# Earlier decay loads and scans, smaller constants, shared masks and a new order in a state-space layer with a GELU MLP

## The chip, the cores and the metric

The kernel runs on one core of a Trainium2 chip. The metric is the device time of one execution in microseconds (us); less is better. The profile is one execution taken by the hardware profiler. Engines are TensorE (PE; its weight loads PEld), VectorE (DVE), ScalarE (ACT), GpSimd (POOL) and SyncE (SP), the last of which only issues transfers here.

## The reference, cut to what matters

Four sequences of 768 steps, 8 heads, head size 32, state size 16. Each head runs a state-space recurrence with a decay `a` per step; its output, regrouped to 3072 tokens of 256 numbers, goes through an MLP with GELU (256 to 2048 to 256). Per chunk of steps:

```python
log_a = np.log(np.clip(a, 1e-06, 1.0))
cum = np.cumsum(la, axis=-1)
L = np.exp(cum[:, :, :, None] - cum[:, :, None, :]) * causal
M = np.einsum('bhin,bhjn->bhij', Cc, Bc) * L
y = M @ xc + (Cc @ state) * exp(cum)
state = exp(sum(la)) * state + sum_j B_j x_j * exp(cum[-1] - cum_j)
...
h = x @ w_in
g = 0.5 * h * (1.0 + np.tanh(c * (h + 0.044715 * h * h * h)))
out = g @ w_out
```

Inputs and output are float32; inside, matmul operands are bf16.

## The kernel before, in words

A chunk is 128 steps, so there are 24 chunks (`gc` or `c`), six to a sequence, handled as 12 pairs (`u`). There are no loops that set the order: every piece of work is a named `Step`, and the string `ORDERED` at the top lists all steps in the order in which they are issued. `name:A`, `:D`, `:P`, `:S` choose ScalarE, VectorE, GpSimd or SP for a step that allows it, and `~n` puts in fill matmuls of `n` x 128 zero columns that only keep TensorE busy. Each engine runs its own steps in that order and waits where it needs another's result. SP holds nearly all loads and stores, in list order too. Buffers are few: two PSUM banks `hp` (first-layer results, also used for state products), one `o_ps`, one `yb`, and two pairs `ga`, `gb` for the score matrices.

**Decays.** Rather than logarithms the kernel scans products. For batch 0's first four chunks `aq_t` holds 128 decays per row; `f_clipq` clips them, `f_Rq` (L331) scans from the end of the chunk, `f_tpq` (L342) turns the result, `f_recip0` (L348) inverts it. `f_mulb` (L416) and `f_mulc` (L409, two halves by parity of the head) multiply B and C by these, TensorE transposes them (`f_tw`), `f_ew` copies them to SBUF. All other chunks use `a_t` (rows of 384 decays): `f_clip`, `f_R`, `f_tp2`, `f_tp6`, `f_recip`. `f_peq`/`f_ppq`/`f_pendq` and `f_pe`/`f_pp`/`f_pend` make the whole-chunk decays through a small matmul with the selector `selp`.

**Per pair.** `G.u` makes the scores C B of both chunks into `ga` and `gb` (L595). `M.u.0` and `M.u.1` (L605, VectorE) multiply them by the triangular mask `tri`. In pair 0 the second half goes another way: `GE.g` (L610, ScalarE) copies one bank `gb` to SBUF, `ME.g` (L616, GpSimd) cuts it with an affine select. `D.u` (or `XD.u`, L573, in pairs 0 and 1) makes the state update, `S.u.k` (L674, L676) adds it to the decayed state, `SP.c` (L683) spreads the state over a block mask as the operand of the next chunk. `Y.u` (L650 and L659) sums both parts into `yb`, and `yev.u` copies it to `xm`. In pairs 0 and 1 x comes as `x4_t` with four steps to a row; `XX.u` (L563) spreads it with the constant `unp`.

**MLP.** `s1.u.i` (L709) makes 256 of 2048 hidden units for the pair's 256 tokens, with two weight halves; `gelu.u.i` (L713, ScalarE) applies GELU; `s2.c.q` (L727) adds a quarter of the second layer for a chunk; `oev.c` copies and `store.c` stores the result. The weights arrive as float32 in four quarters each (`load_wi.q`, `load_wo.q`, 512 KB each) and are cast in halves by `wi.q.k` and `wo.q.k` on any of three engines (the copies of L314, L316, L318). A group `s1.u.i` needs quarter `i // 2` of w_in, `s2.c.q` needs quarter `q` of w_out.

The constants `ident`, `tri`, `m8`, `bmask` and `cz` (zeros that `f_mulc` fills by halves) come from GpSimd, `wz`, `ends`, `unp`, `selp`, `m4` and `par` from VectorE.

Of the kernel before, what the change touches and what calls it, by code (L numbers as in the profile page):

```python
# [8 lines left out]
FP32 = mybir.dt.float32  # L9
BF16 = mybir.dt.bfloat16  # L10
# [77 lines left out]
def kernel(  # L88
# [53 lines left out]
    def a_rows(t, n):  # L142
        return bass.AP(tensor=a.tensor, offset=a.offset + t, ap=[[S, batch * H], [1, n]])
# [14 lines left out]
    def load_aq(i, eng):  # L158
        (nc.scalar if eng == "ACT" else nc.sync).dma_start(out=aq_t[32 * i:32 * i + 32], in_=a_rows(i * Q, Q))  # L159
# [93 lines left out]
    def c_cz():  # L253
        nc.gpsimd.memset(cz, 0.0)
# [708 lines left out]
```

## Time and profile before

| | |
|---|---|
| times of the runs shown | 116.7, 116.92, 117.4 us; median 116.92 |
| span of the profiled execution, first to last instruction | 115.1 us |
| instructions in it | 3372 |
| bytes read and written | 11.04 MB, 3.93 MB |
| VectorE busy | 68.7 us in 135 instructions |
| ScalarE busy | 75.1 us in 149 |
| GpSimd busy | 15.1 us in 32 |

The profiled execution is known by its span. The times of the runs include what lies before the first and behind the last instruction as well: 1.8 us for the median. A row of a timeline has start, duration, engine, line, operation, output and inputs, number of instructions, and in brackets how long the engine had been idle before it and who ended that. A row of a stretch has for each engine busy time and number of instructions, then the granted TensorE clock, the share of the 16 DMA engines and GB/s. Lines are those of the kernel before.

### The profile page before, as it was taken

To read this page: it belongs to the slowest core of one execution; us is meant where nothing else is said; L and a number is where in the kernel's file an instruction comes from. 1 tells how busy PE (TensorE), PEld (TensorE's weight loads), DVE (VectorE), ACT (ScalarE), POOL (GpSimd) and SP (SyncE) were. 2 spreads that over 40 slices of the span, in tenths; PEclk is the share of its full clock that TensorE was granted. 3 is DMA by queue.
4 is the path that set the end of the run, shared out by engine and by line. 5 is a ranking of instruction groups with operands and counts; after the bars stand their busy time and mean duration, and the time that the engine had idled before them with its cause. 6 is when DMAs were issued, how large, how long until landed. Compare 5 with 4: busy or idle time off the path is not lost.

```text
span 115.1 us, 3372 instructions
## 1 busy us (share of the span) xinstructions
PE 109.4 (95%) x1425; PEld 92.2 (80%) x1425; DVE 68.7 (60%) x135; ACT 75.1 (65%) x149; POOL 15.1 (13%) x32
## 2 busy tenths in 40 slices
PE   6999799999999999999999999999999999999990
PEld 2354578978877979799898998998989989999970
DVE  6688799998799989196966281546827421000100
ACT  3119889978657767657576486377766765685710
POOL 6564274122220000020002000000000000000000
PEclk9999999999999999999999999999999999999999
DMA  2999999949969828959478760000014014001132
GB/s 65 236 280 286 397 293 311 278 84 218 225 109 226 214 64 203 192 147 265 102 158 184 174 178 0 6 0 0 0 50 138 0 49 139 0 0 51 46 103 79
DMA packets 43006, 15.97 MB, mean 139 GB/s; under 512 B 36656, under 2 KB 41456, under 8 KB 42992
## 3 DMA queue, kind: packets, MB, share of 16 engines
q1 hardware_dynamic: 42848, 15.68, 53.9%
q8 instruction: 11, 0.18, 0.6%
q10 hardware_dynamic: 144, 0.08, 0.4%
q14 instruction: 3, 0.02, 0.1%
HBM read 11.04 MB, written 3.93 MB: 130 GB/s over the span
## 4 chain that ended last, share of the span: by engine, by line
PE 82%; DMA 8%; SPq 4%; POOL 1%; issue 1%; ACT 0%
PE hp L709 36%; PE o_ps L727 33%; DMA wf<-in_moe_w_out_dram 8%; PE yb L727 3%; PE ga L595 3%; PE yb L650 2%; PE yb L659 2%; SPq L190 1%; PE hp L628 1%; SPq L162 1%; SPq L159 1%; SPq L150 1%; POOL w_out_sb L316 1%; POOL w_in_sb L316 1%; SPq L183 1%
## 5 line engine op out<-in xcount | busy, mean ns | idle before, releaser
L713 ACT ACTIVATE gT<-hp 128x512 bf16<-128x512 f32 x96 | 53.3, 595 | 24.5 <-PE hp L709 24.0
L709 PE MATMUL hp<-xm,w_in_sb 128*128 128x256 bf16 x384 | 51.9, 273 | 0.5 <-ACT pend L314 0.3
L727 PE MATMUL o_ps<-w_out_sb,gT 128*128 128x256 bf16 x352 | 46.4, 273 | 0.0
L709 PEld LDWEIGHTS <-w_in_sb 128*128 128x128 bf16 x384 | 41.2, 114 | 3.2 <-issue 1.7
L727 PEld LDWEIGHTS <-gT 128*128 128x128 bf16 x384 | 37.0, 98 | 4.7 <-issue 0.8
L318 DVE COPY o_sb<-o_ps 128x256 f32<-128x256 f32 x7 | 3.0, 424 | 22.4 <-PE o_ps L727 18.4
L605 DVE TENSOR_TENSOR m<-ga,tri 128x1024 bf16<-128x1024 f32 x12 | 14.6, 1216 | 0.0
L605 DVE TENSOR_TENSOR m<-gb,tri 128x1024 bf16<-128x1024 f32 x11 | 13.4, 1219 | 0.5 <-PE gb L595 0.5
L697 PE MATMUL yb<-wz 128*128 128x512 bf16 (+2 forms) x24 | 8.2, 491 | 1.1 <-DVE warm L222 1.1
L314 ACT ACTIVATE o_sb<-o_ps 128x256 f32<-128x256 f32 x15 | 5.6, 382 | 4.1 <-PE o_ps L727 3.0
L683 DVE SCALAR_TENSOR_TENSOR sp_new<-s_new,pend,bmask 128x256 bf16<-128x256 f32 x17 | 8.0, 479 | 0.1
L316 POOL CAST x<-x_t 128x512 bf16<-128x512 f32 x5 | 3.2, 648 | 34.9 <-DMA x_t<-in_x_dram 22.9
L676 DVE SCALAR_TENSOR_TENSOR s_new<-s_new,pend,hp 128x64 f32<-128x64 f32 x13 | 3.6, 279 | 5.7 <-PE hp L628 5.5
L697 PEld LDWEIGHTS <-wz 128*128 128x128 bf16 x25 | 2.9, 126 | 5.0 <-issue 3.6
L659 PE MATMUL yb<-m,x 128*32 128x128 bf16 x192 | 6.1, 219 | 0.0
L650 PE MATMUL yb<-ce,sp_new 128*32 128x128 bf16 x160 | 5.3, 220 | 0.0
L595 PE MATMUL ga<-ce,bh 32*128 32x256 bf16 x48 | 4.7, 272 | 0.1
L314 ACT ACTIVATE xm<-yb 128x512 bf16<-128x512 f32 x8 | 4.8, 597 | 0.0
L595 PE MATMUL gb<-ce,bh 32*128 32x256 bf16 x48 | 4.7, 273 | 0.0
L727 PE MATMUL yb<-w_out_sb,gT 128*128 128x256 bf16 x32 | 4.1, 273 | 0.0
L659 PEld LDWEIGHTS <-x 128*32 128x32 bf16 x192 | 3.8, 97 | 0.4 <-issue 0.2
L650 PEld LDWEIGHTS <-sp_new 128*32 128x32 bf16 x160 | 3.0, 96 | 1.0 <-issue 1.0
(108 smaller groups left out, 78.4 us busy)
## 6 DMA issues: line engine op xcount, KB each, us to landing
out_dram<-o_sb SPq DMA_DIRECT2D x24, 128.0 KB, 2.0
x_t<-in_x_dram SPq DMA_DIRECT2D x20, 128.0 KB, 3.8
wf<-in_moe_w_in_dram SPq DMA_DIRECT2D x4, 512.0 KB, 8.3
wf<-in_moe_w_out_dram SPq DMA_DIRECT2D x4, 512.0 KB, 8.9
bc_t<-in_B_dram SPq DMA_DIRECT2D x3, 384.0 KB, 4.8
bc_t<-in_C_dram SPq DMA_DIRECT2D x3, 384.0 KB, 4.3
scr<-bc SPq DMA_DIRECT2D x4, 192.0 KB, 3.1
x_t<-in_x_dram SPq DMA_DIRECT2D x1, 512.0 KB, 4.8
```

Of the source, the lines that this page charges most:

```text
L314: nc.scalar.activation(o, i, AF.Copy)
L316: nc.gpsimd.tensor_copy(out=o, in_=i)
L595: nc.tensor.matmul(out=gbank(g)[:, 256 * k:256 * k + 256], lhsT=bh_of(2 * u + k)[gs], rhs=ce_of(2 * u + k)[gs], start=True, stop=True, til ...
L605: nc.vector.tensor_tensor(out=m_of(u)[:, 2 * i:2 * i + 2].rearrange("p g k e t -> p (g k e) t"), in0=gx[i].rearrange("p g (k t) -> p (g k) ...
L650: nc.tensor.matmul(out=y4[32 * j:32 * j + 32, k, w], lhsT=sp[:, 32 * h:32 * h + 32], rhs=ce_of(gc)[:, h % 2], start=first(j), stop=False, ...
L659: nc.tensor.matmul(out=y4[32 * j:32 * j + 32, k, w], lhsT=X16[u][:, k, 32 * h:32 * h + 32], rhs=m[:, h // 2, h % 2, :], start=first(j), st ...
L676: nc.vector.scalar_tensor_tensor(out=s_new, in0=state[("s", gc - 1)], scalar=pend_of(gc), in1=d, op0=ALU.mult, op1=ALU.add)
L683: nc.vector.scalar_tensor_tensor(out=sp_new.rearrange("p (g d) -> p g d", g=4), in0=(XN[0][:, H * D:H * D + 64] if gc == 0 else state[("s" ...
L697: nc.tensor.matmul(out=t[:, 0:m * 128], lhsT=wz, rhs=w3.to_broadcast([128, m, 128]), start=True, stop=True, skip_group_check=True)
L709: nc.tensor.matmul(out=hp[:, j * T:(j + 1) * T], lhsT=w_in_k[:, w, q, k], rhs=xm[:, w, u * T:(u + 1) * T], start=(w == 0), stop=(w == 1))
L713: nc.scalar.activation(gts[u][:, 2 * i:2 * i + 2], hps.pop((u, i)).rearrange("p (j t) -> p j t", j=2), AF.Gelu_apprx_tanh)
L727: nc.tensor.matmul(out=ops[gc], lhsT=gts[u][:, fi, k * Q:(k + 1) * Q], rhs=w_out_sb[:, fi, :], start=(fi == 0 and (u > 0 or k == 0)), stop ...
```

## The change

The new list orders nearly every step anew. Beside the order it does this:

- `aq_t` is loaded by two transfers of 64 rows, both on ScalarE's queue, in place of four of 32 rows (two on ScalarE's queue, two on SP's). Rows that nobody reads now hold other decays. `load_a.0` and `load_a.1` are SP's first two transfers, ahead of C, B and x; `load_a.0` was on ScalarE's queue.
- SP's order of the weights was wi0 wi1 wi2 wo0 wi3 B1 wo1 C1 wo2 wo3 (B1, C1: batch 0's last two chunks); it becomes wi0 wi1 wi2 wo0 C1 B1 wo1 wi3 wo2 wo3.
- The clip of `a_t` stands ahead of `recip0`, and its scan `R`, with `pe` and `tp2`, stands ahead of pair 0's masks. The first half of C's products goes to GpSimd.
- `unp` is cleared by a step of its own and filled by one strided copy in place of four.
- Pair 1 gets the same treatment as pair 0: `GE.1.2`, `GE.1.3` on ScalarE, `ME.1.3` on GpSimd, `ME.1.2` on VectorE.
- `SP.3`, `SP.6`, `SP.7`, `SP.8`, `SP.10` are made by GpSimd in two instructions.
- `s1.1.0` no longer depends on `s1.0.7`, and pair 1's groups are interleaved with pair 0's.
- The fill matmuls are `~39 ~5 ~5 ~5 ~3`; they were `~53 ~9 ~8 ~2 ~13` and a `+4` ahead of `s1.0.2`.
- Both casts of w_in's first quarter are on GpSimd (they were on ScalarE), and both of w_out's third quarter (they were on ScalarE and GpSimd).

```diff
+GEU = (0, 1)
 ORDERED = """
+c_wz load_aq.0:A load_a.0:S load_aq.1:A c_ident c_unp0:D c_zero c_warm c_unp c_sel c_m4 clipq
+load_a.1:S Rq tpq clip load_bc0.1 recip0 peq ~39 ppq pendq:A c_bmask c_tri c_cz:P c_m8 mulc.0:P ~5
+tw.1 ew.1.1:A ew.0.1:A R mulc.1:D ~5 tw.2 pe tp2 load_bc0.0 mulb:P tw.0 ew.0.2:A ew.0.0:A load_x4
+x4.1:P pp G.0 x4.0:D ew.1.2:A ew.1.0:A load_wi.0 load_wi.1 ~5 XX.0 XD.0 recip1 M.0.0 xn.0:D SP.0
+S.0.0 GE.0.2 ME.0.2:P GE.0.3 G.1 xn.1:A GE.1.3 pend:A GE.1.2 ME.0.3:P ~3 Y.0 yev.0.0.2:A load_wi.2
+load_wo.0 load_bc1.1 load_bc1.0 load_wo.1 load_wi.3 load_wo.2 load_wo.3 load_bc.1.1 load_bc.1.0
+load_x.2 load_x.3 wi.0.1:P wi.0.0:P ME.1.3:P wi.1.0:P wi.2.1:P wi.2.0:P wo.0.0:P wo.0.1:P wi.1.1:A
+S.0.1 M.1.0 XX.1 XD.1 S.1.0 ME.1.2:D S.1.1 SP.1:D SP.2:D c_par tp6.2 mul1.1 mul1.0 SP.3:P tp6.1
+wo.1.1:P xn.2:A s1.0.0 gelu.0.0 xn.3:A s1.0.1 gelu.0.1 s1.0.2 gelu.0.2 Y.1 s1.0.3 yev.1.0.2:A
+gelu.0.3 s1.0.4 gelu.0.4 s2.0.0.0.o s1.1.0 gelu.1.0 s2.0.1.0.o T1.1 T1.0 s1.0.5 s1.1.1 wi.3.1:P
+ce1.0:A tp6.3 wo.1.0:D ce1.1:D wi.3.0:D gelu.0.5 bh1:A s2.0.0.1.o s1.1.2 G.2 gelu.1.1 wo.2.0:P
+wo.2.1:P gelu.1.2 s1.0.6 wo.3.0:P wo.3.1:P gelu.0.6 s1.0.7 s2.0.1.1.o gelu.0.7 s1.1.3 gelu.1.3
+s2.0.0.2.o tp6.0 M.2.0 s1.1.4 s1.1.5 N1 s2.0.1.2.o gelu.1.4 bn1:A s1.1.6 s2.0.0.3.o gelu.1.5
...
     def load_aq(i, eng):
-        (nc.scalar if eng == "ACT" else nc.sync).dma_start(out=aq_t[32 * i:32 * i + 32], in_=a_rows(i * Q, Q))
+        (nc.scalar if eng == "ACT" else nc.sync).dma_start(
+            out=aq_t[64 * i:64 * i + 64],
+            in_=bass.AP(tensor=a.tensor, offset=a.offset + 8 * P4 * i, ap=[[P4, 8], [S, H], [1, Q]]))
...
-        for r in range(R4):
-            nc.vector.tensor_copy(out=unp[:, r, :, r], in_=sub)
+        d = unp[:, 0, :, 0]
+        diag = bass.AP(tensor=d.tensor, offset=d.offset, ap=[list(d.ap[0]), [Q + 1, R4], [R4, P4]])
+        nc.vector.tensor_copy(out=diag, in_=sub.rearrange("p (o q) -> p o q", o=1).to_broadcast([128, R4, P4]))
...
-    def f_SP(gc):
+    def f_SP(gc, eng):
         sp_new = st.tile([128, 256], BF16, name="sp_new")
+        if eng == "POOL":
+            sc = spf[gc % 2]
+            nc.gpsimd.tensor_scalar(out=sc, in0=state[("s", gc)], scalar1=pend_of(gc + 1), scalar2=None, op0=ALU.mult)
+            nc.gpsimd.tensor_tensor(out=sp_new.rearrange("p (g d) -> p g d", g=4),
+                                    in0=sc.rearrange("p (o d) -> p o d", o=1).to_broadcast([128, 4, 64]),
+                                    in1=bmask.rearrange("p (g d) -> p g d", g=4), op=ALU.mult)
+            state[("sp", gc)] = sp_new
+            return
...
-        if u:
+        if u not in GEU:
             Mn[u].append(add("D", f_M, u, 1, deps=[g, ctri]))
...
-                s.deps.append(s1.get((u - 1, NI - 1)))
+                s.deps.append(s1.get((u - 1, NI - 1)) if u > 1 else None)
```

138 lines of the change are left out of this document (67 added, 71 removed).

## The prediction

> **What bounds the kernel now.** I read the page's busy times first, then the chain of work that ended last.
>
> ```profile
> PE 109.4 (95%) x1425; PEld 92.2 (80%) x1425; DVE 68.7 (60%) x135; ACT 75.1 (65%) x149; POOL 15.1 (13%) x32
> PE 82%; DMA 8%; SPq 4%; POOL 1%; issue 1%; ACT 0%
> ```
>
> The chain is TensorE (PE) for 82% of the span; the DMA's 8% is one w_out quarter, and nothing else matters. So the question is when TensorE becomes busy for good. The stretches view, cut at the first MLP matmul and at the last hole, says it:
>
> ```profile
> core 0: us, PE busy (x) PEld busy (x) DVE busy (x) ACT busy (x) POOL busy (x), PEclk, DMA share, GB/s
> 14.18:17.51 3.33, 2.83 (x23) 2.24 (x22) 3.33 (x6) 3.03 (x7) 2.29 (x4) 1.00 1.04 286
> 17.51:112.07 94.56, 94.56 (x1243) 84.03 (x1243) 54.90 (x95) 64.58 (x125) 5.58 (x9) 1.00 0.50 118
> ```
>
> From 17.51 to 112.07 us TensorE is busy for all 94.56 us. The change alters no useful matmul, so the time can only move by what TensorE loses before that point, by a new hole behind it, or by fewer costly switches. Before it the timeline of PE has these rows:
>
> ```profile
> 9.08 0.28 PE L595 MATMUL ga<-ce,bh 32*128 32x256 bf16 x2
> 12.27 0.30 PE L659 MATMUL yb<-m,x 128*32 128x128 bf16 x8
> 14.18 1.03 PE L709 MATMUL hp<-xm,w_in_sb 128*128 128x256 bf16 x8 [0.28 <-ACT pend L314]
> 15.67 1.03 PE L709 MATMUL hp<-xm,w_in_sb 128*128 128x256 bf16 x8
> 16.54 0.60 PE L727 MATMUL o_ps<-w_out_sb,gT 128*128 128x256 bf16 x4
> 16.98 0.27 PE L709 MATMUL hp<-xm,w_in_sb 128*128 128x256 bf16 x1
> 18.39 0.29 PE L650 MATMUL yb<-ce,sp_new 128*32 128x128 bf16 x8
> ```
>
> and the chain, later, has these two pieces:
>
> ```profile
> 41.84 0.56 PE hp L709 x4
> 42.39 0.87 PE o_ps L727 x8
> ```
>
> The first useful MLP matmul (s1.0.0) starts at 14.18. Eight MLP matmuls take 0.87 us in a full stream, so one takes 0.109 us. Up to 17.51 come 8 + 8 + 4 + 1 = 21 of them, 2.3 us of work in 3.33 us: **1.0 us is lost** after the start, and all until 14.18 is start-up.
>
> **What the start consists of.** The decay chain of batch 0, from the DVE, POOL and ACT timelines:
>
> ```profile
> 2.41 0.94 POOL L254 MEMSET cz<- 128x1024 bf16 x1
> 2.41 1.25 DVE L271 TENSOR_REDUCE sel<-ident 128x8 f32<-128x128 bf16 x1
> 5.16 0.23 DVE L328 TENSOR_SCALAR acq<-aq_t 128x128 f32<-128x128 f32 x1 [0.89 <-DMA aq_t<-in_a_dram]
> 5.42 0.42 DVE L331 TENSOR_TENSOR_SCAN rq_t<-acq,ends 128x128 f32<-128x128 f32 x1
> 6.37 0.34 DVE L348 RECIPROCAL pt<-rt 128x32 f32<-128x32 f32 x1
> 6.37 1.05 POOL L416 TENSOR_TENSOR bc0s<-bcf,rt 128x512 bf16<-128x512 f32 x1 [1.74 <-DVE rt L342]
> 6.80 1.24 DVE L409 TENSOR_TENSOR cz<-bcf,pt 128x256 bf16<-128x256 f32 x2
> 9.51 1.23 DVE L605 TENSOR_TENSOR m<-ga,tri 128x1024 bf16<-128x1024 f32 x1
> 9.55 1.09 ACT L610 ACTIVATE ge<-gb 128x512 bf16<-128x512 f32 x2
> 11.60 0.94 DVE L331 TENSOR_TENSOR_SCAN r_t<-ac,ends 64x384 f32<-64x384 f32 x1
> 11.78 1.15 ACT L314 ACTIVATE w_in_sb<-wf 128x512 bf16<-128x512 f32 x2 [0.19 <-DMA wf<-in_moe_w_in_dram]
> 12.82 0.18 DVE L387 TENSOR_TENSOR pe<-pe,m 64x24 f32<-64x24 f32 x1
> 12.83 0.37 ACT L314 ACTIVATE x<-hp 128x256 bf16<-128x256 f32 x1
> 13.10 0.59 ACT L314 ACTIVATE xm<-yb 128x512 bf16<-128x512 f32 x1
> 13.16 0.61 POOL L316 CAST w_in_sb<-wf 128x512 bf16<-128x512 f32 x1 [1.72 <-DMA wf<-in_moe_w_in_dram]
> 18.14 0.99 DVE L342 STREAM_TRANSPOSE rt<-r_t 32x64 f32<-32x64 f32 x4
> ```
>
> VectorE waits 0.89 us for the fourth decay load. Its reduction of 2.41 lasts 1.25 us because the fill of cz runs on GpSimd beside it until 3.35; I read that as the two sharing a way to memory.
>
> **The change, part by part.**
>
> *Decay loads.* Two loads on ACT's queue replace two there and two on SP's; all of a goes ahead of C, B, x. The issues before:
>
> ```profile
> 0.80 0.91 ACTq L159 DMA_DIRECT2D aq_t<-in_a_dram  x2
> 1.32 1.03 SPq L159 DMA_DIRECT2D aq_t<-in_a_dram  x2
> ```
>
> SP's second aq load left at about 1.8 (two in 1.03 from 1.32) and the data were used at 5.16. The last one now leaves on ACT as that queue's second issue, at about 1.25 (two in 0.91 from 0.80), half a us sooner, with nothing large ahead of it: ready at 3.5 to 4.5. C leaves behind two a_t issues, about 1.0 us later; for that second only the small loads flow, and I estimate that C, B, x and all weights shift by 0 to 0.8 us and take 0.4.
>
> *Constants.* Three of four copies into unp go, and the clearing of unp is first. VectorE is then free at about 3.1 instead of 4.27, but GpSimd's fill of cz now stands behind ident, bmask and tri, at some 3.1 to 4.05, right where the clip would run. I take the clip at 4.05 (as early as 3.5 if the two don't clash).
>
> *Scans early.* In front of recip0 now stands the clip of the whole a (0.35 by its row, quoted below), behind it the long scan, 0.94. From the clip of 5.16 to the end of recip0 were 1.55 us; with 0.1 to 0.35 more it ends at 5.7. GpSimd then makes half of C's products (half of 1.05 for half the elements, say 0.6, to 6.35) and B's (1.05, to 7.4). VectorE scans to 6.85 and makes the other half of C's, 0.62 of the 1.24 that both took, somewhat stretched beside GpSimd: to 7.7. B's products are done at 7.4, as in the old trace at 7.42; so the transposes and G.0 win almost nothing (8.9 against 9.08). Then pe (two steps of 0.18 at most), tp2 (row 18.14) and x4.0 (0.4, a cast of 512 columns) hold M.0.0 to 9.65 against 9.51. **So the 1.1 us that the loads win are spent on the early scan.** What it buys comes later: pe, pend and the 0.94 scan no longer stand between Y.0 and s1.0.0.
>
> *Masks.* M.0.0 ends at 10.9, G.1 follows; SP.0 (0.48, a row below), behind xn.0 (0.37), ends at 11.7, so Y.0 starts at 11.75 (12.27 before). ScalarE now also makes the copies of pair 1 (2 x 0.55, as in the 9.55 row) and pend ahead of Y.0's copy: it is free at 12.6, and xm is done at 13.2 (13.69 before). For pair 1 VectorE drops a mask of 1.23 us and takes a 128x512 mask from SBUF, 0.43 (its cast of that size, below) to 0.61 (half of 1.23); GpSimd takes about 0.61, as for its casts. So Y.1 goes from 18.4 to about 15.6.
>
> *First quarter of w_in.* Its casts go from ScalarE (two in 1.15) to GpSimd, one behind the other: landing 11.8 + 0.4, then 2 x 0.61, gives 13.4. That and xm (13.2) set s1.0.0 at **13.4, 0.8 us sooner**.
>
> *Between start and saturation.* From 13.4 ScalarE has the cast of w_in's second quarter (0.6), xn.2 (0.37), gelu.0.0 (0.55) and xn.3 in a row, and s1.0.1 waits for xn.2 (0.5), s1.0.2 for a gelu (0.2), s2.0.0.0 for GpSimd's two casts of w_out's first quarter (0.35): about 1.1 us lost against 1.0: **+0.1**. Pair 1's s1 no longer waits for pair 0's last; that is what fills TensorE while weights come in.
>
> *GpSimd's SP steps.* SP.3, 6, 7, 8, 10 leave VectorE.
>
> ```profile
> L683 DVE SCALAR_TENSOR_TENSOR sp_new<-s_new,pend,bmask 128x256 bf16<-128x256 f32 x17 | 8.0, 479 | 0.1
> ```
>
> On GpSimd each is two steps; by 1.05 for 512 columns I estimate 0.7 against 0.48. Between SP.3's input and Y.2, its user, stand 28 groups of four MLP matmuls in the new order, and the others have several: cost nothing, and 0.2 to 0.5 us each if that cover were gone.
>
> *Order behind.* The new order has one block fewer in which TensorE goes to the small tiles and back (13 instead of 14 from the first s1 on). The 41.84 piece, four s1 matmuls behind such a block, took 0.56 us against 0.44 in the stream; with as much on entering: **-0.2**.
>
> *The third quarter of w_out.* This is the place where the gain can be lost.
>
> ```profile
> 0.00:19.50 19.50, 16.83 (x226) 9.82 (x227) 15.69 (x46) 12.00 (x27) 10.67 (x25) 1.00 0.90 263
> 9.23 0.35 DVE L328 TENSOR_SCALAR ac<-a_t 64x384 f32<-64x384 f32 x1
> 15.80 0.43 DVE L318 CAST w_out_sb<-wf 128x512 bf16<-128x512 f32 x1
> 22.61 0.61 POOL L316 CAST w_out_sb<-wf 128x512 bf16<-128x512 f32 x1 [3.21 <-DMA wf<-in_moe_w_out_dram]
> 23.67 1.92 PE L727 MATMUL o_ps<-w_out_sb,gT 128*128 128x256 bf16 x16
> ```
>
> It landed at 22.6, was cast by two engines and used at 23.67, with no hole. The work that stands ahead of that use is the same in the new order, less N1 (0.11). From 13.4: 12 s1 and 4 s2 groups (16 x 0.44 = 7.0), Y.1, T1, G.2 and their switches (1.3, estimated from the blocks' sizes), 1.1 lost: TensorE arrives at 22.8. The same loads stand ahead of that quarter as before, 5.14 MB with it (w_in 2.10, three quarters of w_out 1.57, x 0.52, B and C 0.79, a 0.16), and 263 GB/s had moved 5.13 MB by 19.5; so its landing is not bandwidth, and could be anything from 19.9 to 23.0 with the shift of 0.4. Both casts are now GpSimd's, 1.22 us. I take 21.8, between, so 23.0: **+0.2**.
>
> *Sum:* -0.8 + 0.1 - 0.2 + 0.2 = **-0.7 us**, 114.4 of span against 115.1. The median of the runs shown is 116.92, 1.8 above that span; I carry the difference over: **116.2 us**.
>
> **The rivals.**
>
> *The gain is used up at the start* (no change). If the fill of cz clashes longer, or C's and B's products on both engines stretch each other (one of VectorE's two took twice the other), or the weights shift by the full 0.8, s1.0.0 starts at 13.9 to 14.2 and with the block saved the time is 116.5 to 116.9; I say 116.8. For it speaks that G.0 wins nothing in my sum.
>
> *TensorE waits for w_out's third quarter* (slower). From a landing of 22.6 + 0.4 and two casts in line it starts s2.0.0.2 at 24.2 instead of 23.67, with N1 still to do: +0.65, less the 0.2 of the block: 117.4; a landing one more us late gives 118.4. It decides from a landing of about 22.5 on. For it: that quarter did land at 22.6, and small 128-byte pieces of C and B now stand ahead of w_out's second quarter. Against: three us of that landing were not bandwidth.
>
> *TensorE's clock stays low.* The fills at the start:
>
> ```profile
> 1.05 5.76 PE L697 MATMUL yb<-wz 128*128 128x512 bf16 x14 [1.05 <-DVE warm L222]
> 10.40 0.88 PE L697 MATMUL yb<-wz 128*128 128x512 bf16 x4
> ```
>
> 14 take 5.76 us, 0.41 each, and later four take 0.88, 0.22 each: half speed first, though the clock column says 1.00. The change cuts the first fill to ten, 4.2 us, with holes behind it. If speed comes only after s1 has run for some us, the 3.5 us from 13.4 on do half their work: +1.7 on the forecast, 117.9. [...]
>
> **Chances.** Forecast 0.45 (its own range 115.6 to 116.6); used up at the start 0.25; w_out 0.20; clock 0.10. About 0.5%, 0.6 us, is what a measurement of this kernel can tell from no change. The forecast's 0.45 is faster for 0.37 and same for 0.08; the first rival same for 0.19, faster and slower for 0.03 each; w_out slower for 0.18, same for 0.02; the clock slower. Faster 0.40, same 0.29, slower 0.31. Range **115.5 to 118.0**: down to s1.0.0 at 12.7 (no shift, no clash), up past the w_out case and the clock's.
>
> **What would show it.** Right: first clip at about 4.0; s1.0.0 at 13.2 to 13.6; Y.1 near 15.6; s2.0.0.2 at 22.8 to 23.2 with a hole of at most 0.3 us before it; TensorE full from there. Wrong: s1.0.0 at 13.9 or later; a hole at s2.0.0.2 released by GpSimd's cast; fills or small matmuls at half speed beyond 7 us; a hole before Y.2 or a later Y released by an SP step.

## The result and the profile after

The changed kernel took **120.21 us** (median of 4 runs, 119.36 to 120.47) beside 117.16 for the kernel before on the same chip (116.70 to 117.43): 2.7% slower, ratio 1.0271 with a 95% interval of 1.0212 to 1.0329. The forecast was 116.2 and the range ended at 118.0. The profiled execution spans 118.5 us, against 115.1. Medians here and below count every execution, and some kernels have executions over 1.5% slower than their own fastest, so the spread is given where a reading needs it.

First the stretches view of the changed kernel (columns as in the prediction: busy time of PE, PEld, DVE, ACT, POOL with instruction counts, then the granted TensorE clock, DMA share, GB/s):

```profile
4.00:6.00 2.00, 0.72 (x4) 0.16 (x2) 0.31 (x2) 0.15 (x1) 0.54 (x4) 1.00 1.13 253
6.00:8.00 2.00, 0.57 (x3) 0.55 (x4) 1.97 (x6) 0.00 (x0) 0.64 (x1) 0.83 1.04 291
8.00:10.00 2.00, 1.86 (x13) 1.01 (x11) 1.90 (x4) 0.81 (x3) 2.00 (x3) 0.50 0.99 272
...
18.00:20.00 2.00, 2.00 (x32) 1.28 (x33) 1.94 (x6) 1.73 (x4) 1.92 (x4) 0.50 0.87 225
20.00:22.00 2.00, 2.00 (x32) 1.60 (x25) 1.96 (x4) 1.42 (x4) 1.21 (x3) 0.75 0.96 368
22.00:24.00 2.00, 2.00 (x23) 1.93 (x22) 1.04 (x3) 1.70 (x4) 1.28 (x3) 1.00 1.06 358
```

From 4 to 8 us TensorE is busy for 1.29 us of 4; then the clock falls to 0.50 and stays there until it rises again between 20 and 22, though from 8 on PE reads as 93 to 100% busy. The trace's clock records give the edges: half speed from 7.33 to 20.98 us. PE's timeline has the same in durations:

```profile
1.04 3.68 PE L717 MATMUL yb<-wz 128*128 128x512 bf16 x10 [1.04 <-DVE wz L223]
7.43 0.59 PE L368 MATMUL hp<-peq,selp 128*128 128x4 f32 x2 [2.71 <-DVE peq L363]
11.20 0.39 PE L607 MATMUL ga<-ce,bh 32*128 32x256 bf16 x2
14.67 0.40 PE L671 MATMUL yb<-m,x 128*32 128x128 bf16 x8
16.74 2.79 PE L729 MATMUL hp<-xm,w_in_sb 128*128 128x256 bf16 x12
19.46 0.40 PE L662 MATMUL yb<-ce,sp_new 128*32 128x128 bf16 x8
27.05 0.60 PE L747 MATMUL o_ps<-w_out_sb,gT 128*128 128x256 bf16 x4
```

The ten fills end at 4.72, and TensorE then waits 2.71 us for VectorE's peq. G.0 comes at 11.20 (9.08 before), Y.0 at 14.67 (12.27), s1.0.0 at 16.74 (14.18), Y.1 at 19.46 (18.39). Twelve MLP matmuls take 2.79 us, 0.23 each, where a full stream needs 0.109. The last row is s2.0.0.2: it has no bracket, so it waited for nothing.

Why peq is late stands in the timelines of ACT's queue and SP's queue, of DVE and of POOL:

```profile
0.79 1.84 ACTq L161 DMA_DIRECT2D aq_t<-in_a_dram x2
```

```profile
0.79 0.86 SPq L166 DMA_DIRECT2D a_t<-in_a_dram x2
1.71 0.51 SPq L152 DMA_DIRECT2D bcf<-in_C_dram x1
```

```profile
5.65 0.23 DVE L340 TENSOR_SCALAR acq<-aq_t 128x128 f32<-128x128 f32 x1 [2.64 <-DMA aq_t<-in_a_dram]
7.29 0.94 DVE L343 TENSOR_TENSOR_SCAN r_t<-ac,ends 64x384 f32<-64x384 f32 x1
8.16 0.78 DVE L421 TENSOR_TENSOR cz<-bcf,pt 128x256 bf16<-128x256 f32 x1
8.87 1.00 DVE L397 TENSOR_TENSOR pe<-ac,r_t 64x3 f32<-64x3 f32 x1
9.97 0.47 DVE L399 TENSOR_TENSOR pe<-pe,m 64x24 f32<-64x24 f32 x1
11.99 1.16 DVE L617 TENSOR_TENSOR m<-ga,tri 128x1024 bf16<-128x1024 f32 x1
```

```profile
7.36 1.30 POOL L421 TENSOR_TENSOR cz<-bcf,pt 128x256 bf16<-128x256 f32 x1 [2.67 <-DVE pt L360]
8.62 1.23 POOL L428 TENSOR_TENSOR bc0s<-bcf,rt 128x512 bf16<-128x512 f32 x1
```

The first clip runs at 5.65, not at 4.05: the two loads took 1.84 us to issue (1.19 and 0.62 singly), so the second left at 1.98, behind C's of 1.71. And two pairs of rows overlap in a telling way. GpSimd's product starts at 7.36 inside VectorE's scan (7.29 to 8.23) and ends 0.43 us behind that scan; VectorE's pe, 64x3, starts at 8.87 inside GpSimd's product (8.62 to 9.85) and ends 0.02 behind it, 1.00 us for what took 0.15 before.

How much of the end this explains can be counted in the timelines: MLP matmuls that had started by 22, 30 and 100 us are 53, 108 and 659 of 768 before, and 24, 90 and 629 after. At 22 us 29 are missing, at 30 us 18 (the new order puts other work elsewhere), at 100 us 30: 30 x 0.109 = 3.3 us, nearly all of the difference of the spans, 3.4 us. Behind 22 us TensorE has no hole and full clock in both kernels (busy for 93.00 of 93.00 us from 22 to 115 in the changed one, for 94.56 of 94.56 from 17.51 to 112.07 before, the clock at 1.00), so **all of it is lost by 22 us.**

### The profile page after: what moved, and what is told of

Read it like the earlier page. It is cut to its first block, busy times and chain, and to the rows that moved or that the text cites. A ratio compares the mean times of both kernels' runs of the same rounds, so it can differ in the third digit from the quotient of the medians.

```text
span 118.5 us, 3369 instructions
## 1 busy us (share of the span) xinstructions
PE 111.5 (94%) x1417; PEld 93.2 (79%) x1417; DVE 67.4 (57%) x128; ACT 73.9 (62%) x145; POOL 25.7 (22%) x48
## 4 chain that ended last, share of the span: by engine, by line
PE 90%; DMA 3%; POOL 1%; DVE 1%; ACTq 1%; issue 1%; ACT 0%; DVEq 0%
PE hp L729 38%; PE o_ps L747 33%; PE ga L607 4%; DMA aq_t<-in_a_dram 3%; PE yb L747 3%; PE yb L671 3%; PE yb L662 3%; PE yb L717 1%; POOL cz L421 1%; ACTq L161 1%; PE hp L437 1%; PE hp L575 1%; PE o_ps L575 1%; PE hp L640 1%; PE hp L405 0%
## 5 line engine op out<-in xcount | busy, mean ns | idle before, releaser
L729 PE MATMUL hp<-xm,w_in_sb 128*128 128x256 bf16 x384 | 53.2, 279 | 0.0
L747 PE MATMUL o_ps<-w_out_sb,gT 128*128 128x256 bf16 x352 | 47.0, 273 | 0.0
L729 PEld LDWEIGHTS <-w_in_sb 128*128 128x128 bf16 x384 | 41.7, 115 | 3.1 <-issue 1.2
L617 DVE TENSOR_TENSOR m<-gb,tri 128x1024 bf16<-128x1024 f32 x10 | 12.1, 1212 | 0.2 <-PE gb L607 0.2
L717 PE MATMUL yb<-wz 128*128 128x512 bf16 (+2 forms) x17 | 6.3, 511 | 1.0 <-DVE wz L223 1.0
L671 PE MATMUL yb<-m,x 128*32 128x128 bf16 x192 | 6.8, 235 | 0.0
L703 DVE SCALAR_TENSOR_TENSOR sp_new<-s_new,pend,bmask 128x256 bf16<-128x256 f32 x12 | 5.7, 478 | 0.1
L717 PEld LDWEIGHTS <-wz 128*128 128x128 bf16 x17 | 2.0, 137 | 3.9 <-issue 2.7
L328 POOL CAST w_out_sb<-wf 128x512 bf16<-128x512 f32 x7 | 4.7, 696 | 0.9 <-DMA wf<-in_moe_w_out_dram 0.9
L697 POOL TENSOR_SCALAR spf<-s_new,pend 128x64 f32<-128x64 f32 x5 | 2.4, 475 | 10.9 <-DVE s_new L688 7.1
```

The source lines that it names most:

```text
L328: nc.gpsimd.tensor_copy(out=o, in_=i)
L617: nc.vector.tensor_tensor(out=m_of(u)[:, 2 * i:2 * i + 2].rearrange("p g k e t -> p (g k e) t"), in0=gx[i].rearrange("p g (k t) -> p (g k) ...
L671: nc.tensor.matmul(out=y4[32 * j:32 * j + 32, k, w], lhsT=X16[u][:, k, 32 * h:32 * h + 32], rhs=m[:, h // 2, h % 2, :], start=first(j), st ...
L703: nc.vector.scalar_tensor_tensor(out=sp_new.rearrange("p (g d) -> p g d", g=4), in0=(XN[0][:, H * D:H * D + 64] if gc == 0 else state[("s" ...
L717: nc.tensor.matmul(out=t[:, 0:m * 128], lhsT=wz, rhs=w3.to_broadcast([128, m, 128]), start=True, stop=True, skip_group_check=True)
L729: nc.tensor.matmul(out=hp[:, j * T:(j + 1) * T], lhsT=w_in_k[:, w, q, k], rhs=xm[:, w, u * T:(u + 1) * T], start=(w == 0), stop=(w == 1))
```

## The experiments

Four theories: (1) TensorE's clock, lost in the start-up's holes; (2) decays that land later, not sooner; (3) a longer start-up chain on VectorE and GpSimd; (4) the new order of weights and pieces of B and C on SP. A fifth came up on the way: (5) a later load, `bn`. Numbers behind a ratio are its 95% interval. Each set of runs stands beside its own runs of the kernel before (medians 117.06, 117.10, 117.29, 117.22 and 117.42). "Half speed" is by the clock records of the profiled execution. Diffs show the pieces of `ORDERED` that change.

**E1, a longer first fill in the changed kernel.**

```diff
-peq ~39 ppq
+peq ~75 ppq
```

> The changed kernel with one number changed: the first fill has 75 units of 128 columns in place of 39, so that TensorE has work nearly until the selector matmul at 7.4 us. Theory 1 (clock): most of the 3 us lost comes from TensorE at half clock from 7.3 to 21.0 us, entered because it had nothing to do from 4.7 to 7.4 us. Then the granted clock stays at 1.0, the first MLP matmul comes at about 15.0 us in place of 16.74, and the time is 117.3 to 118.3 us. Theory 2 (late decays) and theory 3 (products on GpSimd and the early scan are slower than forecast) leave the clock out: then the time stays within 0.5 us of 120.2.

119.89 us, 1.0229 (1.0183 to 1.0274). The first hole shrinks from 2.71 to 0.87 us, but holes of 0.61, 0.30 and 0.28 follow, and the clock falls at 10.59 instead of 7.33, until 20.83; s1.0.0 at 16.68. Covering one hole only moves the fall.

**E2, the first decays as four old loads, all on ScalarE's queue**

```diff
-            out=aq_t[64 * i:64 * i + 64],
-            in_=bass.AP(tensor=a.tensor, offset=a.offset + 8 * P4 * i, ap=[[P4, 8], [S, H], [1, Q]]))
+            out=aq_t[32 * i:32 * i + 32],
+            in_=bass.AP(tensor=a.tensor, offset=a.offset + i * Q, ap=[[S, batch * H], [1, Q]]))
...
-load_aq.1:A c_ident
+load_aq.1:A load_aq.2:A load_aq.3:A c_ident
```

> The changed kernel with aq_t loaded by four transfers of 32 rows of the old form, all four on ScalarE's queue; the rest as in the changed kernel. Theory 2 (late decays): the two transfers of 64 rows take longer to issue and to land; with the old form the first clip starts at about 4.6 us in place of 5.65, and all behind it, the first MLP matmul too, comes 0.8 to 1.1 us sooner: 119.1 to 119.4 us with the clock still low from about 7 to 20 us. If theory 1 also feeds on this (the hole on TensorE shrinks from 2.7 to 1.7 us), the clock may stay up and the time falls to 117.5 or less. If the form of the load doesn't matter, 120.2 us.

120.13 us, 1.0275 (1.0234 to 1.0316); clip at 5.97, later still. The four issues took 1.97 us. So it isn't the form of the loads; the theory as expected here fell.

**E3, both of these (first fill 65).**

> Both edits: four transfers of 32 rows on ScalarE's queue, and a first fill of 65 units. Theories 1 and 2 together: clock 1.0, first MLP matmul at about 14.0 us, time 116.3 to 117.2 us. If theory 3 (GpSimd's product at 1.30 us where 0.6 was forecast, VectorE's small step held up to 1.0 us beside it) weighs more, it stays 0.5 us or more above the kernel before, at 117.7 to 118.3 us.

119.51 us, 1.021 (1.012 to 1.0301); the profiled execution 118.64, with half speed only from 15.27 to 18.68 and s1.0.0 at 15.79, though its clip came at 6.01. Of the four executions the two with this mean clock (0.985) took 118.6 and 118.7, the others (0.957) 120.3 and 121.0: clock and time go together.

**E4, the old kernel with a short first fill.**

```diff
-peq ~53 ppq
+peq ~30 ppq
```

> The kernel before with one number changed: its first fill has 30 units in place of 53, so that TensorE has nothing to do from about 4.3 us to its selector matmul at 6.7 us. Theory 1: the clock falls or never rises in the start-up, TensorE runs at half clock until the MLP matmuls have been dense for some us, and the time is 118.5 to 120 us. Theories 2 and 3: the order and the loads are the old ones, so the time stays at 117.2 us.

118.41 us, 1.0124 (1.0067 to 1.0181): a hole of 2.04 us at 4.4, full clock only from 9.98, s1.0.0 at 14.99. **This alone, with every load and step in its old place, costs 1.35 us.**

**E5, the changed kernel with fills in every hole of the start.**

```diff
-peq ~39 ppq
+peq ~80 ppq
...
-mulc.0:P ~5 tw.1 ew.1.1:A ew.0.1:A R mulc.1:D ~5 tw.2
+mulc.0:P ~14 tw.1 ew.1.1:A ew.0.1:A R mulc.1:D ~10 tw.2
...
-x4.1:P pp G.0
+x4.1:P ~5 pp G.0
...
-load_wi.1 ~5 XX.0
+load_wi.1 ~13 XX.0
...
-GE.0.3 G.1
+GE.0.3 ~5 G.1
...
-ME.0.3:P ~3 Y.0
+ME.0.3:P ~10 Y.0
```

> The changed kernel with fill matmuls in every hole that the runs so far showed ahead of the first MLP matmul: first fill 80 instead of 39 columns of 128, and 14, 10, 5, 13, 5, 10 where it has 5, 5, none, 5, none, 3. No useful work is moved. Theory 1 (the clock falls because TensorE idles in the start-up, and the half clock from 7.3 to 21 us is most of the 3 us): TensorE stays at full clock from some 4 to 7 us on, s1.0.0 starts at 15.6 to 15.8 instead of 16.7, and the time is 117.5 to 118.3, 2 us or more below the changed kernel. Theory 3 (the start-up chain is longer by itself, and the clock only follows it): s1.0.0 still at 16.2 or later, 119.3 to 120.2. Both can hold in part: what is left above 117.1 at full clock belongs to the chain.

The profiled execution took 117.41 us at full clock from 5.07 to the end, with s1.0.0 at 14.94: the clock can be held. It is the fastest of the six, though; the others took 118.87 to 121.3, the median is 119.45, 1.0212 (1.0158 to 1.0265). Four of these others have a mean clock of 1.00 too, but that alone doesn't say that it was held (E9 reads 1.00 with half speed until 18.43). E11's profile does: 119.06 us at full clock from 4.90. So something else costs time as well; E6, E11 and E12 show a part of it.

**E6, E5 with both of C's products on VectorE and the long scan, its transposes and pend late.**

```diff
-Rq tpq clip load_bc0.1 recip0
+Rq tpq load_bc0.1 recip0
...
-mulc.0:P ~14 tw.1 ew.1.1:A ew.0.1:A R mulc.1:D ~10 tw.2 pe tp2 load_bc0.0 mulb:P tw.0 ew.0.2:A ew.0.0:A load_x4
+load_bc0.0 mulc.0:D mulc.1:D mulb:P ~10 tw.1 tw.0 ew.0.0:D ew.0.1:A tw.2 ew.0.2:A load_x4
...
-XD.0 recip1 M.0.0 xn.0:D SP.0 S.0.0 GE.0.2
+XD.0 clip M.0.0 xn.0:D SP.0 S.0.0 R pe GE.0.2
```

> As the run with fills in every hole, and beside that both of C's products are on VectorE again and the long decays' clip, scan, pe, transposes and pend stand late, as in the kernel before (clip and scan after XD.0 and S.0.0, tp2 after SP.2). Theory 3 (GpSimd's product of 1.3 us ahead of B's, and VectorE's pe held beside GpSimd, cost the start some 1.5 us): bc0s is done about 1.2 us sooner after recip0, G.0 at 9.6 to 10.0 instead of about 11, s1.0.0 at 14.4 to 14.9, and the time is 0.8 to 1.5 us below the run with fills alone. If the early scan and the split were not what is late: the same time within 0.3 us.

119.39 us, 1.0221 (1.0169 to 1.0273): no gain. This version put the small product of pe on TensorE ahead of s1.0.0, and it waited 1.35 us for VectorE there, and s1.0.0 came at 16.13; at 51 us it waits another 1.24 for a load (the row stands at E11). What the run does show is the chain ahead of that: from the clip (5.42) to G.0 (9.85) 4.43 us, against 5.25 in E5 (5.15 to 10.40). **GpSimd's product and the early scan cost G.0 0.82 us** in these two profiles.

**E7, E6 with the decays loaded as in the kernel before.**

```diff
-load_aq.0:A load_a.0:S load_aq.1:A c_ident
+load_aq.2:A load_bc0.1 load_aq.1:S load_aq.3:S load_aq.0:A c_ident
...
-clipq load_a.1:S Rq tpq load_bc0.1 recip0 peq ~80
+clipq load_bc0.0 load_x4 Rq tpq load_a.0:A load_a.1:S recip0 peq ~64
```

> As the run with fills, products on VectorE and the late scan, and beside that the decays are loaded as in the kernel before (C first on SP, four loads of 32 rows over both queues, the long decays behind the transposes); first fill 64. Theory 2 (the decays come later in the changed kernel because both of its loads wait in ScalarE's queue): first clip at 5.0 to 5.3 instead of 5.65, s1.0.0 0.4 to 0.6 us sooner than in the run without this, and the time 0.3 to 0.6 below it. If the way they are loaded is worth nothing: the same clip within 0.1 and the same time within 0.3.

119.63 us, 1.0221 (1.0178 to 1.0264). The clip came at 4.98, 0.44 sooner, and s1.0.0 0.43 sooner, as expected; the time did not follow, with half speed from 17.07 to 20.49 behind the same 1.35 us hole. At 51 us TensorE waits 0.27 us for the same load as in E6.

**E8, E5 with the old order of weights.**

```diff
-load_bc1.1 load_bc1.0 load_wo.1 load_wi.3 load_wo.2
+load_wi.3 load_bc1.0 load_wo.1 load_bc1.1 load_wo.2
```

> As the run with fills in every hole, and beside that w_in's last quarter and w_out's second are issued ahead of batch 0's second B and C as in the kernel before. Theory 4 (the 128-byte pieces of B and C ahead of the weights hold SP's queue and delay the third and fourth quarter): w_in's last quarter lands at 19 to 20 instead of 21.7, s1.0.6 and all behind it come sooner, and the time is 0.4 to 1.0 below the run with fills alone. If weights aren't what TensorE waits for: the same within 0.3 us.

119.85 us, 1.0212 (1.0151 to 1.0273), at full clock from 3.76 on and with s1.0.0 at 15.15. At 20.4 TensorE waits 1.40 us for VectorE's products of the second B and C, and at 23.3 another 0.52 for a cast of w_out: the new order of work needs B and C as early as the new load order brings them. Theory 4 fell.

**E9, the old kernel without any fill.**

```diff
-~53 ~9 ~8 ~2 ~13 s1.0.2+4
+s1.0.2
```

> The kernel before without any of its fill matmuls; nothing else is changed, and no load or useful instruction moves in the order. Theory 1 (TensorE's low clock is most of the changed kernel's 3 us): here too the clock is low through the whole start-up, until some 17 to 21 us, though the loads, the scans and the masks are the old ones; the time is 119.0 to 120.0, 2 to 3 us above the kernel before, and the changed kernel's rest above it, 0.2 to 1.2 us, belongs to the longer chain. The rival (the clock is worth no more than the 1.35 us that the shortened first fill showed in the old kernel, and the other 1.7 us come from the chain): 118.2 to 118.7.

119.71 us (118.66 to 120.18), 1.0194 (1.0141 to 1.0247). In its profiled execution, the fastest, the first record of full clock is at 18.43; the clock column counts from that record on and reads 1.00 before it, so the durations on PE's timeline must tell:

```profile
9.69 0.40 PE L595 MATMUL ga<-ce,bh 32*128 32x256 bf16 x2 [0.47 <-ACT ce L314]
15.80 3.17 PE L709 MATMUL hp<-xm,w_in_sb 128*128 128x256 bf16 x16 [0.28 <-ACT pend L314]
19.25 1.04 PE L709 MATMUL hp<-xm,w_in_sb 128*128 128x256 bf16 x8
25.18 0.28 PE L595 MATMUL ga<-ce,bh 32*128 32x256 bf16 x2
```

The same score matmul takes 0.40 at 9.7 and 0.28 at 25, and 16 MLP matmuls take 3.17 us where 8 take 1.04 later. **The old kernel at half speed until 18.4 us loses 2.4 us**, with no step moved. The clip stayed at 5.16.

**E10, E6 with the small product behind s1.0.1.**

```diff
-Y.0 pp pend:A yev.0.0.2:A
+Y.0 yev.0.0.2:A
...
-s1.0.1 gelu.0.1 s1.0.2
+s1.0.1 gelu.0.1 pp pend:A SP.3:P s1.0.2
```

> As the run with fills, products on VectorE and the late scan, with one slip mended: there the product of the long decays' end (pp) stood on TensorE ahead of the first MLP matmul and waited 1.35 us for VectorE; here it stands behind s1.0.1, and pend and SP.3 behind it. Theory 3: s1.0.0 at 14.4 to 14.9 where the clip comes at 5.0 to 5.5, and the time 1.0 to 1.4 us below that run, 117.9 to 118.4. If the split product and the early scan cost nothing: s1.0.0 no sooner than the 14.94 of the run with fills alone, and the time within 0.4 us of that run's 119.45.

121.05 us, 1.0334 (1.028 to 1.0388), the slowest of all: waits of 0.76 us (for VectorE's s_new) and 1.05 (for ScalarE's copy of x) now stand around s1.0.0, and the clock falls at 19.19. A miss: it settles nothing but that a step moved off one wait met the next.

**E11, E5 with a first fill of 64.**

> As the run with fills in every hole, with a first fill of 64 instead of 80. That run took from 117.4 to 120.1 us without a fall of the clock. If this is because a fill takes 0.41 us at half clock and 0.22 at full, so that a late clock makes the first fill itself late (20 matmuls would end at 8.2 instead of 6.7): with 16 it ends by 7.3 even so, and the times stand closer together, 117.4 to 118.8, though a run in which the clock comes early can have a hole ahead of the second product and fall, 119 to 120. If the spread has another cause: the same spread and the same median within 0.4 us.

119.55 us, 1.0181 (1.0132 to 1.023). Full clock from 4.90 to the end, s1.0.0 at 15.39, four executions still at 119.1 to 119.7 and two at 121.8 and 122.2. The first fill's length isn't what sets the median. But its profile has a hole that the changed kernel's has not, far behind the start. PE's timelines of E6, of E11, of E12 (next), and of the changed kernel at that step, the state update of batch 1, which needs `bn` read back from scratch:

```profile
51.54 0.24 PE L640 MATMUL hp<-x,bn 128*32 128x64 bf16 x8 [1.24 <-DMA bn<-scr]
```

```profile
50.07 0.24 PE L640 MATMUL hp<-x,bn 128*32 128x64 bf16 x8 [0.80 <-DMA bn<-scr]
```

```profile
52.08 0.30 PE L640 MATMUL hp<-x,bn 128*32 128x64 bf16 x8 [3.15 <-DMA bn<-scr]
```

```profile
51.32 0.24 PE L640 MATMUL hp<-x,bn 128*32 128x64 bf16 x8
```

E5's profile, the 117.41, has no such wait: there the load of bn left at 43.96, in E6, E11 and E12 at 46.4 to 46.7. Why it leaves sooner in one execution than in another wasn't looked into.

**E12, a version put together from the above**: the changed masks, constants and later order; two old loads of the first decays on each queue, ahead of C and B; both of C's products on VectorE; the long scan behind them.

```diff
-c_wz load_aq.0:A load_a.0:S load_aq.1:A c_ident
+c_wz load_aq.0:A load_aq.1:S load_aq.2:A load_aq.3:S load_bc0.1 c_ident
...
+load_bc0.0 load_a.0:A load_a.1:S Rq tpq recip0 peq ~72 ppq pendq:A c_bmask c_tri c_cz:P c_m8 mulc.0:D mulc.1:D mulb:P
+tw.1 ew.0.1:A clip R tw.0 ew.0.0:A tw.2 ew.0.2:A pe load_x4 x4.1:P ~5 G.0 x4.0:D ew.1.1:A ew.1.2:A ew.1.0:A
+load_wi.0 load_wi.1 pp ~13 XX.0 XD.0 M.0.0 xn.0:D SP.0 S.0.0 GE.0.2 ME.0.2:P GE.0.3 ~5 G.1 xn.1:A
...
+SP.1:D SP.2:D c_par tp2 recip1 tp6.2
```

> A version put together from what the runs showed: the changed kernel's masks, small constants and later order; the four old loads of the first decays ahead of C and B on both queues; both of C's products on VectorE with B's on GpSimd beside them; the long decays' clip and scan behind these products but ahead of the first mask; fills in the holes (first fill 72). If the chain's lateness (GpSimd's product ahead of B's, the loads) and the clock are the two causes: clip at 4.8 to 5.2, G.0 at 9.0 to 9.5, s1.0.0 at 13.6 to 14.2, TensorE at full clock from some 7 us on, and 116.2 to 117.2 us, at or below the kernel before. If the masks, the later order or the weights' order carry a cost of their own: 117.6 or more with s1.0.0 at 14.2 or sooner.

118.05 us, 1.0048 (0.9999 to 1.0096). Clip at 3.32, G.0 at 8.71, s1.0.0 at 14.24; four of six executions at 117.5 to 118.1. The profiled one took 122.3, with the hole of 3.15 us above and half speed for 3.4 us behind it.

**E13, E14, E15: bn's load moved forward**, in the changed kernel, in E5 and in E12.

```diff
-turn_s.2.1 turn_s.2.0 load_bc.3.1 load_x.8 load_s.2
+turn_s.2.1 load_s.2 turn_s.2.0 load_bc.3.1 load_x.8
```

> The changed kernel with one load moved: batch 1's bn (read back from scratch) is issued on SP right behind the first transposed load instead of behind the second, batch 3's C and two x loads. Theory 5 (this load is a second bound that the late start hides: in the changed kernel it is issued at 46.7, its user comes at 51.3 and doesn't wait; where the start is mended the user comes at 48.4 to 50 and waits 0.8 to 3.2 us): no change here, 119.9 to 120.5 us, with no hole at 50 us. If bn's lateness is part of the changed kernel's 3 us as it stands: 0.5 us or more faster.

> The run with fills in every hole (119.45 us, 117.4 to 120.1) with bn's load moved forward in the same way. Theory 5: the wait for bn is what its slower executions lost, so the median falls to 117.2 to 118.0 and they stand close together; TensorE has no hole at 48 to 50 us. If their spread came from the start (clip, clock): no change of the median beyond 0.4 us.

> The version put together before (118.05 us; in its profiled execution TensorE waited 3.15 us for bn at 49 us and its clock fell behind that) with bn's load moved forward. Theory 5: no hole at 49 us, full clock to the end, s1.0.0 at 14.0 to 14.4, and 116.5 to 117.3 us. If bn isn't it: 117.8 to 118.3.

SP's timelines of the kernel before, the changed kernel and E13:

```profile
43.58 0.41 SPq L509 DMA_DIRECT2D bn<-scr x1
```

```profile
46.66 1.14 SPq L521 DMA_DIRECT2D bn<-scr x1
```

```profile
42.43 1.26 SPq L521 DMA_DIRECT2D bn<-scr x1
```

The load leaves 4.2 us sooner in E13, and the time stays: 119.97 (one execution at 118.11, five at 119.8 to 120.5), 1.0158 (1.0075 to 1.0241), an interval that overlaps the changed kernel's. In E14, where the start is held, the median falls from 119.45 to 118.56, 1.0119 (1.0079 to 1.0159), and all six executions lie between 117.9 and 119.0; TensorE has no hole at 49 us. E15: 117.71, 1.0064 (1.0027 to 1.0102), s1.0.0 at 14.03, no hole there. **bn is a second wait that the late start hid**, 0.27 to 3.15 us in four profiles and gone where its load was moved. What it is worth in time isn't settled: E14 is tighter than E5 (117.41 to 121.3), but its fastest isn't faster.

**E16, E15 with more moves in the start** (cz's fill ahead of the clip, x ahead of the long decays, pe and pp later).

```diff
+c_ident c_cz:P c_unp0:D
...
+load_bc0.0 load_x4 load_a.0:A load_a.1:S Rq
...
+x4.1:P ~5 G.0 x4.0:D pe
...
+load_wi.1 ~5 XX.0 XD.0 M.0.0 xn.0:D SP.0
...
+GE.0.3 ~9 G.1 pp xn.1:A
```

> The same with three more moves in the start: the fill of cz stands ahead of the first clip on GpSimd (there it held the clip for 0.94 us), x is loaded ahead of the long decays, and the long decays' pe and its product stand behind XX.0 and G.1 instead of ahead of them (TensorE waited 0.66 us for pe at 9.1 and XX.0 came at 11). If the start is bound by these: clip ends at 3.7 instead of 4.26, M.0.0 at 9.2 to 9.6, Y.0 at 11.9 to 12.3, s1.0.0 at 13.0 to 13.5, and 115.4 to 116.4 us, faster than the kernel before. If C's, B's and w_in's landings bind it instead: s1.0.0 at 13.8 or later, within 0.4 us of the run without these moves.

119.44 us, 1.0154 (1.0098 to 1.0209). The clip was done at 3.62, but the long decays, now behind C, B and x, landed at 8.39; M.0.0 went to 11.40 and the clock fell at 11.79. A miss, of the change's own kind: a load moved behind larger ones.

**E17, the old kernel with its four decay loads ahead of C; E18, E15 with the long transposes earlier.**

```diff
-load_aq.2:A load_bc0.1 c_tri load_aq.1:S load_aq.3:S load_aq.0:A c_m8
+load_aq.2:A load_aq.1:S load_aq.0:A load_aq.3:S load_bc0.1 c_tri c_m8
```

```diff
-pp ~13 XX.0 XD.0 M.0.0 xn.0:D SP.0 S.0.0 GE.0.2
+pp ~6 XX.0 XD.0 M.0.0 xn.0:D SP.0 S.0.0 tp2 recip1 GE.0.2
```

> The kernel before with one move: the four old loads of the first decays, two on each queue, are all issued ahead of C (there C stands ahead of SP's two). This is the part of the change's idea that its own two loads on ScalarE's queue did not carry out. Theory 2: the first clip starts when VectorE's constants are done, at 4.0 to 4.4 instead of 5.16, and C and B, which come later, bound what follows: G.0 at 8.6 to 8.9 instead of 9.08, s1.0.0 at 13.7 to 14.1, 116.6 to 117.1 us, 0.1 to 0.6 faster than the kernel before. If C's later landing costs more than the clip wins: 117.3 to 117.8.

> The version put together with bn's load moved forward (117.71 us, s1.0.0 at 14.03, a hole of 0.38 us at 20.5 that ends with VectorE's cast of w_out) with two moves: the transposes of the long decays (1.0 us on VectorE) stand behind S.0.0, where VectorE waits for G.1, instead of behind SP.2, and the fill ahead of XX.0 is 6 instead of 13. If what keeps it above the kernel before is VectorE's work at 17 to 21 us and that fill: no hole at 20.5, s1.0.0 at 13.5 to 13.9, and 116.6 to 117.3. If the later order itself costs: the hole moves on or stays, 117.5 to 118.0; a fall of the clock for want of the fill would show as 118 or more.

E17: 117.08, 0.9984 (0.9936 to 1.0032), clip at 4.20, s1.0.0 at 13.79, 0.39 us sooner. By 22 us nothing of that is left, 52 MLP matmuls against 53: at 17.63 (17.51 before) TensorE waits for GpSimd's cast of w_in. E18: 117.50, 1.002 (0.9977 to 1.0062), s1.0.0 at 13.96, the hole at 20.5 gone, but one of 1.04 us, for ScalarE's copy of x, ahead of 15.60, where E15 waited 0.37. Neither can be told from the kernel before, and no version was found that beats it by more than its interval.

## Why the prediction was wrong

**What failed.** The sum had s1.0.0 at 13.4 and no term for TensorE's clock, which was left to a rival. s1.0.0 came at 16.74, and half speed lasted until 20.98. The start was late by the steps *Decay loads* and *Scans early*, and the lateness opened the hole of 2.71 us behind a fill that the change had cut.

**Its basis** (only what TensorE loses before it is full can move the time) held for what happened, by the count of MLP matmuls. It was incomplete as a bound on what could have been won: with the start mended, bn at 49 us is next, and in the old kernel a start 0.39 us sooner is used up by 22 us (E17).

***Decay loads*: the step that failed first.** I had the last load leaving at 1.25 "with nothing large ahead of it" and the clip at 4.05. It left at 1.98, behind C, and the clip ran at 5.65: 1.6 us late (5.15 to 5.95 in the other runs with these loads, 5.16 before). By the rows the place against C decides. In the kernel before two loads leave ahead of C's packets or beside them and two behind; in E18 all four are issued by 1.68, ahead of C at 1.71. E17, which moves only this in the old kernel, has issued SP's two by 1.66, ahead of C at 1.72, and its clip at 4.20 waits for no data. The page's table of issues (before), and E18's clip and queue:

```profile
aq_t<-in_a_dram ACTq DMA_DIRECT2D x2, 16.0 KB, 2.4
aq_t<-in_a_dram SPq DMA_DIRECT2D x2, 16.0 KB, 3.0
```

```profile
0.79 0.87 SPq L161 DMA_DIRECT2D aq_t<-in_a_dram x2
1.71 0.42 SPq L152 DMA_DIRECT2D bcf<-in_C_dram x1
```

```profile
3.36 0.90 DVE L340 TENSOR_SCALAR acq<-aq_t 128x128 f32<-128x128 f32 x1 [0.36 <-DMA aq_t<-in_a_dram]
```

The last column of the table is us from issue to landing: 3.0 where C's issue is ahead on the same queue. E18's view of that tile has

```profile
DMA to landing us min/median/max: 1.7/1.8/1.9
```

The idea of the step was right (clip at 3.3 to 3.5 in E12, E15, E18), this way of doing it was not. Why one issue took 1.19 us was not tried.

***Constants*: right**, though the late clip hid it. VectorE was free at 3.0, and where the data came in time (E18) the clip of 0.23 us took 0.90, until 4.26, just behind the fill of cz (3.19 to 4.14), as the prediction had it; in E16, with that fill moved ahead, it took 0.25. The reduction of 1.25 us took 0.38 in the changed kernel, where the fill no longer runs beside it.

***First quarter of w_in*: right.** GpSimd's two casts took 1.17 us and were done at 14.90, ahead of xm at 16.15.

***Scans early*: wrong.** "Half of C's products 0.6" was 1.30, B's 1.23 behind it; they end 2.6 us after recip0 where I had 1.7. pe's two steps, "0.18 at most" each, took 1.00 and 0.47. In the overlaps shown above the two additions hold each other up: the scan holds GpSimd's product for 0.87 us, and GpSimd's next product holds pe, 1.00 us for 0.15. E5 has the same (scan to 7.74, product to 8.17, 0.43 behind it; pe 1.00), and E6 priced both together at 0.82 us to G.0. I had taken such an overlap for a stretching by some tenths. What makes the one wait for the other was not tried by itself.

***Masks*: right, and the gain larger.** From Y.0 to Y.1 I had 3.85 us (6.1 before); at full clock it was 3.2 in E5 (13.71 to 16.95). They came late because all did. ***SP steps on GpSimd***: sized too small, and hidden, as I said: no hole ahead of a later Y. The changed kernel's groups (count | busy, mean ns of one | idle before) add up to 1.24 us where I had 0.7:

```profile
L697 POOL TENSOR_SCALAR spf<-s_new,pend 128x64 f32<-128x64 f32 x5 | 2.4, 475 | 10.9 <-DVE s_new L688 7.1 <-PE gb L607 3.8
L698 POOL TENSOR_TENSOR sp_new<-spf,bmask 128x256 bf16<-128x256 f32 x5 | 3.8, 763 | 0.4
```

***Order behind***: -0.2 isn't contradicted: E5's s1.0.0 is 0.76 us behind the old one and its span only 0.6. These are two single executions, and the 0.16 takes in all that differs behind s1.0.0, so the term isn't shown by itself. ***The third quarter of w_out***: no wait at 27.05, and none in E15, where s1.0.0 came at 14.03; that rival fell.

**The rival that came true is the clock, with a chance of 0.10.** Its mechanism was right in the main: a first fill cut to ten matmuls, holes behind it, half speed through the first MLP work. (Full speed had come at 3.92, within the fill, and was lost at 7.33.) Its price was too low, 1.7 us for 3.5 us at half speed, because I took the half speed to end once s1 ran; the 3.5 us were an estimate that no run shows. It lasted 13.65 us, and half speed until 18.4 costs even the old kernel 2.4 us (E9). By the clock records the half-speed stretches were 13.65 us here, 10.24 in E1 and 3.41 in E3, four, three and one times 3.41; what sets these lengths was not shown.

**What the 3.05 us consist of**, as excess of each median over its own runs of the kernel before:

| kernel | excess, us | ratio (95%) |
|---|---|---|
| changed | 3.05 | 1.0271 (1.0212 to 1.0329) |
| fills in the holes (E5) | 2.35 | 1.0212 (1.0158 to 1.0265) |
| and bn sooner (E14) | 1.34 | 1.0119 (1.0079 to 1.0159) |
| and loads, products, scan mended (E15) | 0.49 | 1.0064 (1.0027 to 1.0102) |
| and long transposes sooner (E18) | 0.08 | 1.002 (0.9977 to 1.0062) |

So some 1.7 us are the clock, from the changed kernel to E14; E13 and E14, which differ in the fills alone, give 1.4. E5's own row is loose: its two fastest executions took 117.41 and 118.87, so the step from it to E14 is no measure of bn. Some 0.85 are the decays' loads, GpSimd's product and the early scan, all in one step and with intervals that overlap a little, and 0.4 what E18's two moves took away (VectorE's work around 17 to 20 us and a fill), within the intervals' reach. E4 and E9 give the clock's price from the other side. What stays open: how the 0.85 divides between loads and scan, since E6 and E7 lost it in holes of their own (pe's and bn's), what bn is worth in time, and what the later order is worth by itself.

## What to carry to other kernels

Before cutting or moving a start-up step that only fills TensorE, read how long TensorE would idle until the next data and what the granted clock does behind such a hole: in the old kernel a first fill of 30 for 53 alone cost 1.35 us (E4). Look at a load's place among all queues' issues, not at its place in one queue, and whether a large transfer is issued between: the second load of the first decays left at 1.98, behind C at 1.71, and the clip ran at 5.65; with four loads issued by 1.68, ahead of C, it ran at 3.36 (E18). When a late start is mended, look for the next wait at once, in the order of transfers too: here a load moved by 3 us (43.58 to 46.66) showed no wait until the start was repaired.

## What the runs showed of the hardware that was not expected

In E3 the clock fell where PE reads as busier than where it held. Its stretches view:

```profile
8.00:10.00 2.00, 1.36 (x14) 0.74 (x13) 2.00 (x3) 0.66 (x3) 2.00 (x2) 1.00 1.01 307
14.00:16.00 2.00, 1.89 (x67) 1.19 (x67) 1.86 (x5) 1.95 (x5) 2.00 (x5) 0.82 0.76 170
```

From 8 to 10 us TensorE is busy 68% of the time, mostly with fills, and the clock stays; in the stretch from 14 to 16, 94% busy with 67 mostly small matmuls (32x64 and 128x128 tiles among them), it falls at 15.27. The last 0.73 us of that stretch are at half speed, which makes busy time longer (in E9 the same score matmul took 0.40 us at half speed and 0.28 at full). The same view for the 3.41 us ahead of the fall, as long as the half speed behind it, from 11.86, gives 2.61 us busy (77%, 83 matmuls), and for the 3.42 us ahead of those, where the clock stayed, 2.23 (65%, 27 matmuls). The changed kernel stays at half speed for 13.65 us while PE reads, from 8 us on, as 93 to 100% busy. So the profile's busy time of small tiles doesn't tell whether the clock will hold; which measure does, these runs don't show. VectorE's pe, 64x3, took 1.00 us in the changed kernel, in E3 and in E5, each time with a GpSimd product started 0.24 or 0.25 us before it, for 0.15 in the kernel before.
